# Turning the stationary and moving operands of the value product round in the later batches of a banded attention + MLP kernel

## The chip, the cores and the metric

One core of a Trainium2 chip runs the whole program. The metric is the device time of one execution in microseconds (us). The core's engines work side by side, each through its own instruction list in order: TensorE (PE; its weight loads are shown apart, as PEld), VectorE (DVE), ScalarE (ACT), GpSimd (POOL) and SyncE (SP), which issues the DMAs. Matmul results land in PSUM, eight banks of 512 fp32 columns.

## The reference

Attention over 8 batches, 8 heads, 576 positions and 64 head dimensions: each query sees 32 keys, the last 32 in heads 0 to 3 ("plain"), every fourth of the last 128 in heads 4 to 7 ("dilated"). Then a two-layer perceptron over the 4608 rows of 512.

```python
scores = scale * np.matmul(q, k.transpose(0, 1, 3, 2))
mask_plain = (rel >= 0) & (rel < window)
mask_dil = (rel >= 0) & (rel < window * dilation) & (rel % dilation == 0)
...
attn = np.exp(scores - max)
attn = attn / (np.sum(attn, axis=-1, keepdims=True) + 1e-09)
x = np.matmul(attn, v)          # heads side by side: 4608 x 512
...
h = x @ w_in                    # 512 -> 2048
g = np.maximum(0.01 * h, h)
return g @ w_out                # 2048 -> 512
```

## The kernel before

**A list written by a planner.** Every piece of work is a task with an engine, an estimated duration, dependencies and a priority (a due time). `_Plan.run` plays these tasks through and fixes the order in which each engine gets its instructions; the chip then runs each engine's list in order. Batches 0 and 1 are "early" and go another way than batches 2 to 7 ("late", `b >= EARLY`), which the change is about.

**Attention of a late batch.** Heads go in pairs, four pairs (`hp`) to a batch: 2 and 3 dilated, 0 and 1 plain. `load_group` loads q, k and v and casts them to fp16 (POOL); `turn` transposes q and k with DVE (L562, L573) and spreads q with POOL (L567) into `slots`. Then `unit` handles a third of a pair, 384 score columns, three units to a pair:

- scores, keys on partitions and queries in columns: 2 matmuls of 192 columns (L742), or in the small dilated unit 4 of 96 (L726), into the one bank `sps`;
- the exponential on ACT, PSUM to `ee` (L748), and the 0/1 mask on DVE (L762);
- the values: v with 64 columns of ones beside it (128 columns) is the **stationary** operand, the exponentials are **moving**, 4 matmuls of 96 columns (L806) or 8 of 48 (L796). Partitions 0 to 63 of `ops` then hold the unnormalised x with its dimensions on partitions, and partitions 64 to 127 hold the sum of each column, 64 times over;
- the reciprocal of the sums as two ACT instructions over 64 x 384, Ln (L818) and Exp of the negative (L820);
- DVE multiplies and writes into `xt` (L824): two instructions of 64x192 in a plain unit, one of 64x384 in a dilated one.

**The perceptron** works on `chunks` of 384 columns of `xt`, three to a pair of batches. `up` (L851): 16 results per chunk, each 4 matmuls of 384 columns into one of two `hps` banks, each taken away by ACT with the leaky ReLU (L862). The second layer takes 128-row tiles: the first four as plain products (L903), the other 32 in eight groups of four by a scheme of seven products instead of eight (`group`, L993), with sums of the inputs by DVE (L979), evictions by ACT (L1022) and result sums by DVE (L1030). A group uses three cells X, Y and Z, each one bank, out of `fps0`, `fps1` and the `tp` bank; `roles` exchanges the two `fps` banks from group to group. The last group (`split`) has six banks.

**PSUM**: `tp`, two `ops`, two `hps`, `sps`, two `fps`.

Of the kernel before, what the change touches and what calls it, by code (L numbers as in the profile page):

```python
# [23 lines left out]
def _constants():  # L24

    ident = np.eye(128, dtype=np.float16)
    p = np.arange(128)[:, None]
    key = p - 32
    c = np.arange(96)[None, :]
    qry = 4 * (c % 24) + c // 24  # L30
    rel = qry - key
    band = (rel >= 0) & (rel < WIN)
    first = band & (key >= 0)
    rel0 = c - p
    d0 = (rel0 >= 0) & (rel0 < WIN)
    c1 = np.arange(48)[None, :]
    rel1 = 96 + c1 - (16 + p)
    d1 = (rel1 >= 0) & (rel1 < WIN)
    rel2 = 96 + c1 - np.where((p < 64) & (p % 4 == 0), 128 + p // 4, p)
    d2 = (rel2 >= 0) & (rel2 < WIN)  # L40
    masks = np.concatenate([first, band, band, d0, d1, d2], axis=1)
    parts = [ident, np.where(masks, 0.0, -60000.0), masks]
    return np.concatenate([x.astype(np.float16) for x in parts], axis=1)
# [17 lines left out]
class _Plan:  # L61
# [22 lines left out]
    def run(self):  # L84
        free, waiting = {}, {}
# [13 lines left out]
        while len(order) < len(self.tasks):  # L99
# [19 lines left out]
            t.eng, t.start, t.dur = eng, at, dict(t.choices)[eng]  # L119
            free[eng] = at + t.dur  # L120
# [17 lines left out]
def kernel(  # L138
# [10 lines left out]
    nc = tc.nc  # L149
# [39 lines left out]
    NMASK = 288 + 96 + 48 + 48  # L189
    NCON = 128 + 2 * NMASK  # L190
    con = sbuf("con", [128, NCON])
    ident = con[:, 0:128]
    M_PL, M_D0, M_D1, M_D2 = 128, 128 + 288, 128 + 288 + 96, 128 + 288 + 96 + 48
    w_in = sbuf("w_in", [128, NI * DFF])
    w_out = sbuf("w_out", [128, NJ * DM])
    NST, NNAT, NVS, NV, NT, NE, NR, NO, NG = 5, 3, 2, 3, 6, 4, 3, 3, 3
# [3 lines left out]
    vst = [sbuf(f"vst{i}", [128, 2048], FP32) for i in range(NVS)]  # L200
# [6 lines left out]
    ee = [sbuf(f"ee{i}", [128, 384]) for i in range(NE)]  # L207
    rc = [sbuf(f"rc{i}", [128, 384], FP32) for i in range(NR)]
# [8 lines left out]
    t4 = sbuf("t4", [128, 2048])  # L217
# [6 lines left out]
    tpb = bank("tp", FP16)  # L224
    ops = [bank(f"ops{i}") for i in range(2)]
    hps = [bank(f"hps{i}") for i in range(2)]
    banks = {"S": [bank("sps0")], "O": ops}
# [50 lines left out]
    t_bias = load("ACT", con[:, 128:128 + NMASK], const_d[:, 128:128 + NMASK], 128, 2 * NMASK, [],  # L278
                  -1498.5)
    t_con = load("SP", con[:, 128 + NMASK:NCON], const_d[:, 128 + NMASK:NCON], 128, 2 * NMASK, [],  # L280
# [45 lines left out]
    def load_group(b, g, prio, prio_v):  # L326
# [26 lines left out]
        vn, v_old = ring("VST", NVS, v_users := [])  # L353
        vs = vst[vn]
        if dil and early:
            lv = [load("SP", at(vs, 0, 128, 0, [256, 4], [1, 256]),
                       dram(v, base, [4 * D, 128], [HS, 4], [1, 256]), 512, 1024, v_old, prio_v)]
            v_late[b] = vs, v_old, v_users
        elif dil:
            lv = [load("SP", at(vs, 0, 128, i * 256, [512, 4], [1, 256]),  # L360
                       dram(v, base + i * 64 * D, [4 * D, 128], [HS, 4], [1, 256]),
                       512, 1024, v_old, prio_v) for i in range(2)]
        elif early:
            lv = []
            for j in range(2):
# [7 lines left out]
                lv.append(lj)  # L373
        else:
            lv = [load("SP", at(vs, 0, 128, 0, [D, 24], [1, D]),
                       dram(v, base - 32 * D, [D, 128], [96 * D, 24], [1, D]),
                       3072, 256, v_old, prio_v)]

        for j in range(2):
            nn, n_old = ring("NAT", NNAT, n_users := [])  # L380
            na, c_qk = nat[nn], []
            for o in range(2):
# [5 lines left out]
                else:  # L388
# [8 lines left out]
            h_a, h_s = (2 * j * n_v, n_v) if early else (j * n_v, 2 * n_v)  # L397
            n, w = n_v // D, 128 * (8 if dil else 6)
            c_v = [cast(at(vt, 0, 128, 0, [w, 2], [128, n], [1, D]),
                        at(vs, 0, 128, h_a, [h_s, 2], [D, n], [1, D]), 2 * n_v,  # L400
                        (lv[j] if early and not dil else lv) + d_old, prio_v)]
            v_users += c_v
# [70 lines left out]
    segs = {b: [(0, 96, 384 * (b % 2)), (96, 48, 768 + 192 * (b % 2))] for b in range(B)}  # L473
    chunks = [(m, 384 * i, 384) for m in range(B // 2) for i in ((0, 1, 2) if m < 3 else (0, 2, 1))]
# [8 lines left out]
    def chunk_at(m, x):  # L483
        return next(c for c, (mc, xc, n) in enumerate(chunks) if mc == m and xc <= x < xc + n)

    def pieces(b, hp, u, tiled):
# [7 lines left out]
        for u0, nu, base in segs[b]:  # L494
# [14 lines left out]
            if dil and b >= EARLY:  # L509
                p0 = h0 % 2 * 64  # L510
                res.append((key, 0, 64,
                            at(xm, p0, p0 + 64, h0 // 2 * 1152 + x, xs[0], [1152, 2], xs[1]), 0,
                            [cs[0], [step // 2, 2], cs[1]]))
                continue
# [22 lines left out]
    held = {t.name: [] for t in banks["S0"] + banks["O0"]}  # L537
# [8 lines left out]
    def turn(b, hp, part, prio):  # L546
# [11 lines left out]
        if b >= EARLY:  # L558
# [5 lines left out]
            for hh in range(2):  # L564
                p0 = 64 * hh
                t = add("POOL", 0.72, 0.2, [tq] + old + zq,
                        lambda e, p0=p0, hh=hh: nc.gpsimd.tensor_copy(  # L567
                            out=at(qb, p0, p0 + 64, hh * S + o, *od),
                            in_=at(xb, p0, p0 + 64, i, *id_)), prio)
                x_users.append(t)  # L570
                ev.append(t)
# [123 lines left out]
    def unit(b, hp, part, u, turned, prio):  # L695
# [11 lines left out]
        if sk == "S0":  # L707
            held[st.name].append(s_users)
            held[ot.name].append(o_users)
# [4 lines left out]
        def scores(e):  # L714
            if by_pe:
                if small:
                    bias = at(con, 0, 128, M_D2, [0, 8], [1, 48])
                elif dil:
                    bias = at(con, 0, 128, M_D0, [0, 4], [1, 96])
                else:  # L720
                    bias = at(con, 0, 128, M_PL + (0 if u == 0 else 96),
                              [96, 2], [0, 2], [1, 96])
                nc.tensor.matmul(st[:, 0:384], ident, bias, start=True, stop=False)
            if small:
                for s in range(4):
                    nc.tensor.matmul(  # L726
                        st[:, 96 * s:96 * s + 96],
                        (at(kb, 0, 128, s * 144, [1, 128]) if b < EARLY
                         else at(kb, 0, 128, PAD + s + 4 * 16, [4, 128])),
# [3 lines left out]
            for i in range(2):  # L733
                t = 2 * u + i
                if dil:
                    ka = (at(kb, 0, 128, t * 144, [1, 128]) if b < EARLY
                          else at(kb, 0, 128, PAD + t, [4, 128]))
# [14 lines left out]
        def mask(e):  # L752
            if small:
                mk = at(con, 0, 128, NMASK + (M_D2 if b < EARLY else M_D1), [0, 8], [1, 48])
                io = at(et, 0, 128, 0, [48, 8], [1, 48])
            elif dil:
                mk = at(con, 0, 128, NMASK + M_D0, [0, 4], [1, 96])
                io = at(et, 0, 128, 0, [96, 4], [1, 96])
            else:
                mk = at(con, 0, 128, NMASK + M_PL + (0 if u == 0 else 96), [96, 2], [0, 2], [1, 96])  # L760
# [7 lines left out]
        def values(e):  # L768
# [23 lines left out]
            if small:  # L792
                for s in range(4):
                    for hh in range(2):
# [3 lines left out]
                            at(vt, 0, 128, (hh * 8 + 4 * (b >= EARLY) + s) * 128, [1, 128]),  # L798
# [23 lines left out]
        for key, p0, p1, dst, c, i_ in pieces(b, hp, u, tiled):  # L822
# [3 lines left out]
            t_n = add("DVE", 0.61 if dil and b >= EARLY else 0.38, 0.2,  # L826
# [5 lines left out]

    gt_free = {1 - NG: sum(w_used[11:14], []), 2 - NG: w_used[0] + w_used[1]}

    def up(c, j, x, n, done, acc):

        m, x0, n_c = chunks[c]
        if c == 0 and j in WIDE:
            h_users = []
            ht, name, x_r = {2: (fps[1], "F", -1), 3: (banks["S"][0], "S", -1), 4: (ops[0], "O", 0),  # L840
                             5: (ops[1], "O", 1), 6: (tpb.bitcast(FP32), "TP", -1)}[j]
# [6 lines left out]
        def pe(i0, i1):  # L848
            def fn(e):
                for i in range(i0, i1):  # L850
                    nc.tensor.matmul(ht[:, 0:n],  # L851
                                     at(w_in, 0, 128, i * DFF + j // 2 * 256 + j % 2, [2, 128]),
                                     at(xt[m % 2], 0, 128, i * 1152 + x0 + x, [1, n]),
# [16 lines left out]
    def rows(c, tt):  # L870

        m, x0, n = chunks[c]
        res = []
        for p in range(128):
            x = x0 + tt * 128 + p
# [52 lines left out]
    def weight_sums():  # L928
# [7 lines left out]
        minus(4, flat(sums[4]), w_block(1, 0), flat(sums[2]), [t_sum[2]])  # L936
        minus(3, w_block(0, 1), w_block(1, 1), w_block(0, 1), [t_sum[1]] + plain_parts)

    roles = [0, 1]
# [3 lines left out]
    def group(four, acts, at_time, split):  # L943
# [15 lines left out]
        if split:  # L959
            cells = [[(b, 0) for b in pair] for pair in (fps, [trio[2], banks["S"][0]], ops)]  # L960
            pairs = ((0,), (1,))
            room = {fps[0].name: last_of[fps[0].name], fps[1].name: last_of[fps[1].name],
                    trio[2].name: last_of[trio[2].name], banks["S"][0].name: rings["S"][-1],
                    ops[0].name: rings["O"][-2], ops[1].name: rings["O"][-1]}
        else:
            three = [trio[i] for i in roles] + [trio[2]]
            roles.reverse()
            cells = [[(b, HN * i) for i in range(2)] for b in three]
            pairs = ((0, 1),)
            room = {b.name: last_of.get(b.name, first_banks.get(b.name, [])) for b in trio}  # L970
# [6 lines left out]
        def add_up(dst, a, b, op, deps, who, t_late=0.0):  # L977
            t = add((("DVE", 0.66), ("POOL", 2.3)), None, 0.2, deps,
                    lambda e: ENG[e].tensor_tensor(out=dst, in0=a, in1=b, op=op),  # L979
# [5 lines left out]
        def product(src, rhs, cell, first, deps, when, who=None):  # L985
            ts = []
            for i in range(2):
# [9 lines left out]
                old = room.get(bk.name, []) if first else []  # L997
# [35 lines left out]
        def result(make, deps, pair, row, col):  # L1033
            if split:
                r = (row + col) * 2 + pair[0]
                ob, o_old, o_users = vst[0][:, r * HN:r * HN + HN], rings["VST"][-2], []
# [12 lines left out]
        def flat8(i):  # L1049
# [12 lines left out]
        p7 = product(raw(2, 0), lambda j: w_out[:, j * DM + HN:j * DM + DM], Z, True,  # L1062
                     lambda i: [s3[i], t_sum[3]], 2, 2)

# [7 lines left out]
        p6 = product(raw(0, 0), w_sum(2), X, False, lambda i: [s2[i], t_1[i], t_sum[2]], 3, 0)  # L1072
# [24 lines left out]
        if not split:  # L1097
            for b, t in zip(three, (c12, c11, c21)):
                last_of[b.name] = [t[0]]
# [3 lines left out]
    trio = [fps[0], fps[1], tpb.bitcast(FP32)]  # L1103
# [25 lines left out]
    def release():  # L1129

        def users(t):
            return sum(held[t.name], [])
# [4 lines left out]
    def attend(b, part, first, step):  # L1137
        units = {None: (0, 1, 2), 0: (0, 1), 1: (2,)}[part]
        if part == 1:
            load_rest(b, ranks[b])  # L1140
        for n, hp in enumerate((2, 3, 0, 1)):
# [3 lines left out]
            got = turn(b, hp, part or 0, first + step * n)  # L1145
            for u in units:
                unit(b, hp, part or 0, u, got, first + step * n)
# [3 lines left out]
    for m in range(B // 2):  # L1151
# [14 lines left out]
        while n_c < len(chunks) and chunks[n_c][0] == m:  # L1166
# [11 lines left out]
            if n_c == 2:  # L1178
# [5 lines left out]
                for i in range(2):  # L1184
                    first_banks[fps[i].name] = rings["F"][i - 2]
                first_banks[trio[2].name] = rings["TP"][-1]
# [60 lines left out]
```

## Time and profile before

| what | value |
|---|---|
| time, median of 3 runs (lowest, highest) | 315.37 us (313.8, 317.77) |
| the profiled execution: its own time, its span | 316.78 us, 315.0 us |
| mean granted TensorE clock in it | 0.994 |
| DMA | 51.2 MB in 163,395 packets, 140,448 of them under 512 bytes |
| q, k and v of the late batches | 96 loads of 144 KB, 12 of 512 KB, 6 of 768 KB |

The profile is one execution. Busy time of PE is modelled: a matmul's record runs from its start to the arrival of its last result, so records overlap and a busy PE is not yet a PE at its full rate. The full rate shows in the distance between the starts of neighbouring matmuls. In the chain of waits each row has a start, a length and what ran.

### The profile page before, as it was taken

Reading aid. Unit: us, or ns where it says so; the run is one execution under the profiler, and the core shown is the slowest. Engines: PE = TensorE matmul, PEld = TensorE weight load, DVE = VectorE, ACT = ScalarE, POOL = GpSimd, SP = SyncE. Lnnn points to the kernel's source line nnn. Section 1 sums busy time; section 2 is a strip of 40 time slices with the busy share of each in tenths; the row PEclk is TensorE's granted clock in tenths of the full one; section 3 lists DMA queues with packets and bytes.
Section 4 is the critical chain, followed back from the end, with each engine's and each line's share of the span. In section 5 each row is a group of like instructions: output and inputs, shape, how many; then the busy total and the mean of one; then the engine's idle time right before and its main releaser. Section 6 shows DMA issues by size and latency. Waiting matters only on the chain.

```text
span 315.0 us, 7276 instructions
## 1 busy us (share of the span) xinstructions
PE 297.0 (94%) x2622; PEld 216.2 (69%) x2622; DVE 222.7 (71%) x453; ACT 231.9 (74%) x534; POOL 133.9 (43%) x175
## 2 busy tenths in 40 slices
PE   7996999799889998899999999999899999999995
PEld 3644554467778786688777777787687777767784
DVE  5844899755988999987979878779956442151172
ACT  3934864589998899789899998699697885454421
POOL 3558655563564767455655747957200000000000
PEclk9999999799999999999999999999999999999999
DMA  7999999999599932899599978796203010130223
GB/s 252 343 332 397 403 295 197 246 174 205 180 173 200 233 60 73 163 188 245 114 220 184 195 184 140 187 182 168 58 10 92 4 34 2 45 91 0 57 79 100
DMA packets 163395, 51.20 MB, mean 163 GB/s; under 512 B 140448, under 2 KB 160800, under 8 KB 163360
## 3 DMA queue, kind: packets, MB, share of 16 engines
q1 hardware_dynamic: 162336, 50.01, 66.6%
q10 hardware_dynamic: 1024, 0.75, 0.8%
q8 instruction: 20, 0.33, 0.4%
q14 instruction: 15, 0.12, 0.1%
HBM read 41.30 MB, written 9.44 MB: 161 GB/s over the span
## 4 chain that ended last, share of the span: by engine, by line
PE 61%; DVE 14%; DMA 7%; SPq 6%; ACT 6%; issue 4%; DVEq 0%; ACTq 0%
PE hps L851 29%; PE fps L993 18%; SPq L248 6%; PE tp L993 6%; DMA wst<-in_moe_w_in_dram 3%; DVE xt L824 3%; ACT gt L862 3%; DMA stg<-in_q_dram 3%; PE ops L806 2%; PE sps L742 2%; DMA stg<-in_k_dram 2%; DVE slots L532 2%; DVE gt L979 2%; DVE ee L762 2%; DVE rest L979 1%
## 5 line engine op out<-in xcount | busy, mean ns | idle before, releaser
L851 PE MATMUL hps<-xt,w_in 128*128 128x384 f16 (+1 forms) x812 | 149.2, 316 | 5.7 <-ACT gt L862 1.9
L862 ACT ACTIVATE gt<-hps 128x384 f16<-128x384 f32 (+1 forms) x203 | 92.3, 461 | 35.9 <-PE hps L851 33.6
L851 PEld LDWEIGHTS <-w_in 128*128 128x128 f16 x832 | 77.0, 98 | 42.6 <-issue 7.7
L993 PEld LDWEIGHTS <-gt 128*128 128x128 f16 x768 | 73.5, 98 | 12.2 <-DVE gt L979 0.7
L824 DVE TENSOR_TENSOR xt<-ops,rc 64x192 f16<-64x192 f32 (+2 forms) x138 | 52.1, 397 | 24.0 <-ACT rc L820 19.3
L567 POOL COPY slots<-turned 64x576 f16<-64x576 f16 x48 | 36.0, 749 | 52.0 <-DVE turned L562 50.4
L818 ACT ACTIVATE rc<-ops 64x384 f32<-64x384 f32 (+1 forms) x94 | 43.5, 464 | 12.9 <-PE ops L806 4.0
L748 ACT ACTIVATE ee<-sps 128x384 f16<-128x384 f32 x92 | 44.7, 485 | 8.6 <-PE sps L742 4.4
L258 POOL CAST nat<-stg 128x576 f16<-128x576 f32 (+1 forms) x53 | 42.0, 816 | 13.0 <-DMA stg<-in_k_dram 6.5
L993 PE MATMUL fps<-w_out,gt 128*128 128x256 f16 x368 | 47.5, 273 | 0.0
L820 ACT ACTIVATE rc<-rc 64x384 f32<-64x384 f32 (+1 forms) x96 | 46.5, 491 | 1.1
L762 DVE TENSOR_TENSOR ee<-ee,con 128x384 f16<-128x384 f16 x79 | 38.4, 492 | 12.5 <-ACT ee L748 12.0
L1030 DVE TENSOR_TENSOR osb<-tp,stg 128x512 f32<-128x512 f32 x14 | 9.6, 686 | 25.0 <-ACT stg L1022 16.8
L742 PE MATMUL sps<-slots 128*128 128x192 f16 x152 | 25.0, 246 | 0.9 <-DVE slots L532 0.8
L258 POOL CAST vd<-vst 128x1024 f16<-128x1024 f32 (+2 forms) x20 | 19.2, 983 | 6.6 <-DMA vst<-in_v_dram 6.4
L742 PEld LDWEIGHTS <-slots 128*128 128x128 f16 x160 | 15.4, 102 | 8.1 <-DVE slots L532 1.4
L1022 ACT COPY stg<-fps 128x512 f32<-128x512 f32 (+1 forms) x26 | 13.9, 534 | 9.4 <-PE fps L993 9.3
L532 DVE COPY slots<-tp 64x128 f16<-64x128 f16 (+7 forms) x43 | 13.6, 333 | 7.2 <-PE tp L580 6.7
L573 DVE STREAM_TRANSPOSE slots<-nat 128x576 f16<-128x576 f16 x24 | 18.0, 762 | 0.7 <-POOL nat L258 0.6
L562 DVE STREAM_TRANSPOSE turned<-nat 128x576 f16<-128x576 f16 x24 | 18.1, 762 | 0.1
L979 DVE TENSOR_TENSOR gt<-gt 128x1024 f16<-128x1024 f16 x21 | 17.2, 838 | 0.8 <-PE fps L993 0.7
L993 PE MATMUL fps<-wst,gt 128*128 128x256 f16 x128 | 16.4, 273 | 0.0
(102 smaller groups left out, 317.6 us busy)
## 6 DMA issues: line engine op xcount, KB each, us to landing
vst<-in_v_dram SPq DMA_DIRECT2D x14, 512.0 KB, 4.8
stg<-in_q_dram SPq DMA_DIRECT2D x48, 144.0 KB, 3.3
stg<-in_k_dram SPq DMA_DIRECT2D x48, 144.0 KB, 2.9
vst<-in_v_dram SPq DMA_DIRECT2D x6, 768.0 KB, 5.6
gt<-in_moe_w_in_dram SPq DMA_DIRECT2D x5, 512.0 KB, 8.3
out_dram<-osb SPq DMA_DIRECT2D x22, 96.0 KB, 2.0
out_dram<-osb SPq DMA_DIRECT2D x44, 48.0 KB, 1.7
out_dram<-osb SPq DMA_DIRECT2D x27, 64.0 KB, 2.6
```

The lines of the kernel that those rows point to most:

```text
L258: ENG[e].tensor_copy(out=dst, in_=src)
L567: lambda e, p0=p0, hh=hh: nc.gpsimd.tensor_copy(out=at(qb, p0, p0 + 64, hh * S + o, *od), in_=at(xb, p0, p0 + 64, i, *id_)), prio)
L742: nc.tensor.matmul(st[:, 192 * i:192 * i + 192], ka, qa, start=not by_pe, stop=i == 1 or not by_pe)
L748: lambda e: nc.scalar.activation(out=et, in_=st[:, 0:384], func=AF.Exp, scale=SCALE), prio + 0.1)
L762: ENG[e].tensor_tensor(out=io, in0=io, in1=mk, op=ALU.mult)
L818: lambda e: nc.scalar.activation(out=r_out, in_=r_in, func=AF.Ln), prio + 0.2)
L820: lambda e: nc.scalar.activation(out=r_out, in_=r_out, func=AF.Exp, scale=-1.0),
L824: nc.vector.tensor_tensor(out=dst, in0=at(ot, p0, p1, c, *i_), in1=at(rt, p0, p1, c, *i_), op=ALU.mult)
L851: nc.tensor.matmul(ht[:, 0:n], at(w_in, 0, 128, i * DFF + j // 2 * 256 + j % 2, [2, 128]), at(xt[m % 2], 0, 128, i * 1152 + x0 + x, [1, n] ...
L862: lambda e: nc.scalar.activation(out=gt[c % NG][:, j * n_c + x:j * n_c + x + n], in_=ht[:, 0:n], func=AF.Prelu, alpha=0.01),
L979: lambda e: ENG[e].tensor_tensor(out=dst, in0=a, in1=b, op=op),
L993: nc.tensor.matmul(bk[:, x:x + HN], tl[:, off + j * step:off + j * step + 128], rhs(j), start=first and x == 0 and j == 0, stop=j == HJ - ...
```

## The change

For late batches `unit` gives way to `late_unit`, two units of 576 columns to a head pair instead of three of 384, and to `across`, once per group of two pairs. `unit`, with its old operand order, stays for batches 0 and 1.

- The scores of a unit go into two banks (`s_two`, the old `sps` and `tp`), in 6 matmuls of 96 columns (plain) or 2 of 192 and 2 of 96 (dilated). One exponential and one mask cover 576 columns.
- In the value product the **exponentials are stationary** (96 columns: 96 queries) and **v with one column of ones moves** (65 columns). Queries are now on partitions, and the sum is the 65th column. A plain unit has 6 such matmuls, a dilated one 8.
- DVE takes the reciprocal of 96 x 6 sums and multiplies 96 x 384 results with it into `xnat`.
- When a group of four heads is done, `across` turns `xnat` with 12 TensorE transposes (128 stationary columns, 96 moving) into the `ops` banks, and four moves a batch (ACT or DVE, as the planner finds) of 128 x 576 take them to `xt`.
- Without the `tp` bank, a group of the second layer has X on `fps0` and both Y and Z on `fps1`; p7 comes after p6 and waits for the result sum c11 that empties Y.
- v is loaded by head pair in half-size staging slots (8 loads a batch instead of 3, the same bytes), three slots of 1024 columns instead of two of 2048; one of the weight sums moves into that memory.
- `xt` holds a batch's 576 columns together, so a chunk of the third kind reads two runs of 192. Sums of the second layer are planned on DVE alone; the planner lets DVE and POOL work delay one another.

```diff
-    tpb = bank("tp", FP16)
-    ops = [bank(f"ops{i}") for i in range(2)]
+    s_two, o_two = (ps.tile([128, 1024], FP32, name=n) for n in ("sps", "ops"))
+    sps0, tpf = s_two[:, 0:512], s_two[:, 512:1024]
...
+        def values(e):
+            def one(t, hh, c, k, first, last):
+                r = 65 * (2 * t + hh)
+                nc.tensor.matmul(ot[0:96, r:r + 65], et[:, c:c + 96],
+                                 at(vt, 0, 128, (hh * (8 if dil else 6) + k) * 128, [1, 65]),
+                                 start=first, stop=last)
+            for t in range(3):
+                for hh in range(2):
+                    if not dil:
+                        one(t, hh, 288 * hh + 96 * t, 3 * n + t, True, True)
+                    elif t < 2:
+                        one(t, hh, 336 * hh + 240 * t, 2 * n + t, True, True)
+                    else:
+                        one(t, hh, 336 * hh + 96, 4 + 2 * n, True, False)
+                        one(t, hh, 336 * hh + 144, 5 + 2 * n, False, True)
...
+        t_r = add("DVE", 0.13, 0.15, [t_v] + c_old,
+                  lambda e: nc.vector.reciprocal(out=rt[0:96, :], in_=at(ot, 0, 96, 64, [65, 6])),
+                  prio + 0.2)
+        def norm(e):
+            nc.vector.tensor_tensor(
+                out=at(xb, 0, 96, 768 * n + 64 * i, [256, 3], [128, 2], [1, D]),
+                in0=at(ot, 0, 96, 0, [130, 3], [65, 2], [1, D]),
+                in1=at(rt, 0, 96, 0, [2, 3], [1, 2], [0, D]), op=ALU.mult)
...
+    def across(b, g, prio):
+        for i in range(2):
+            def pe(e, i=i, tb=tb):
+                for t in range(6):
...
+                    nc.tensor.transpose(to, xb[0:96, 256 * t + 128 * i:256 * t + 128 * i + 128],
+                                        ident[0:96, 0:96])
+            t_x = move(dst, tb[:, 0:S], S, [t_t] + x_free.get(m, []), prio + 0.2, ("ACT", "DVE"))
...
-            three = [trio[i] for i in roles] + [trio[2]]
-            roles.reverse()
-            cells = [[(b, HN * i) for i in range(2)] for b in three]
+            cells = [[(b, HN * i) for i in range(2)] for b in (*fps, fps[1])]
...
-        p6 = product(raw(0, 0), w_sum(2), X, False, lambda i: [s2[i], t_1[i], t_sum[2]], 3, 0)
+        p6 = product(raw(0, 0), w_sum(2), X, False, lambda i: [s2[i], t_1[i], t_sum[2]], 2, 0)
+        p7 = product(raw(2, 0), lambda j: w_out[:, j * DM + HN:j * DM + DM], Z, True,
+                     lambda i: [s3[i], t_sum[3]], 3, 2,
+                     after=None if split else [c11[0]])
```

## The prediction

> **What bounds the kernel now.** I read the page first. By the shares of busy time PE leads, with ACT and DVE near each other behind it:
>
> ```profile
> PE 297.0 (94%) x2622; PEld 216.2 (69%) x2622; DVE 222.7 (71%) x453; ACT 231.9 (74%) x534; POOL 133.9 (43%) x175
> ...
> PE   7996999799889998899999999999899999999995
> ...
> PEclk9999999799999999999999999999999999999999
> ```
>
> A modelled 94% does not say at what rate PE works, and the stages differ, so I cut the span into windows of 25 us. The columns are the window, its length, busy us (instructions) of PE, PEld, DVE, ACT and POOL, the granted clock, the DMA share and GB/s:
>
> ```profile
> 75.00:100.00 25.00, 22.69 (x253) 19.56 (x250) 21.85 (x42) 23.51 (x68) 14.40 (x19) 1.00 0.89 182
> 100.00:125.00 25.00, 24.84 (x235) 19.04 (x233) 24.03 (x41) 23.05 (x53) 17.07 (x21) 1.00 0.62 131
> 125.00:150.00 25.00, 23.32 (x219) 17.89 (x217) 21.98 (x42) 21.11 (x47) 12.97 (x18) 1.00 0.94 193
> 150.00:175.00 25.00, 24.96 (x227) 18.39 (x225) 22.44 (x39) 23.22 (x53) 13.32 (x16) 1.00 0.91 184
> 175.00:200.00 25.00, 25.00 (x230) 19.48 (x228) 21.01 (x44) 21.64 (x49) 17.95 (x19) 1.00 0.83 156
> ```
>
> From 75 to 225 us late attention and perceptron share the engines, with ACT at 84 to 94% and DVE at 82 to 96%. Third came the chain of waits in order of time, which shows both the rates and the one stretch where PE really stops:
>
> ```profile
> 81.66 0.66 PE hps L851 x8
> 82.32 0.17 PE sps L742 x2
> 82.49 0.87 PE fps L993 x8
> 83.36 0.21 PE ops L796 x8
> ...
> 86.20 0.32 ACT gt L862
> 86.52 0.04 issue
> 86.56 0.49 PE hps L851 x4
> 87.05 0.22 PE sps L742 x2
> 87.27 0.17 PE ops L806 x4
> ```
>
> Eight matmuls of 256 columns take 0.87 us, two of 192 columns 0.17, four of 96 columns 0.17, eight of 48 columns 0.21: PE starts a matmul every 109, 83, 42 and 26 ns, about 0.43 ns a column, and the narrowest not under 25 ns. At 86.2 PE waits for ACT to empty an `hps` bank. Taking each matmul's columns at that rate away from the distance to the next start leaves PE's true gaps (those over 0.1 us): 4.3 us in 50 to 75, 4.3 in 75 to 100, 3.0 in 100 to 150, 0.2 in 150 to 225, 1.7 in 225 to 250, 0.4 later; 13.9 us after 50 us. From 150 us on, apart from one gap, PE runs at its full column rate: **there only PE's own work counts, and an ACT instruction saved is worth nothing.** The change is worth what it takes out of the 13.9 us, less what it adds to PE.
>
> Last, the rows by form, for prices (busy us, mean ns of one, then idle before):
>
> ```profile
> L748 ACT ACTIVATE ee<-sps 128x384 f16<-128x384 f32 x92 | 44.7, 485 | 8.6 <-PE sps L742 4.4 <-PE sps L726 3.6
> L820 ACT ACTIVATE rc<-rc 64x384 f32<-64x384 f32 x80 | 41.2, 516 | 0.9
> L818 ACT ACTIVATE rc<-ops 64x384 f32<-64x384 f32 x80 | 38.9, 487 | 8.7 <-PE ops L806 4.0 <-PE ops L796 2.8
> L762 DVE TENSOR_TENSOR ee<-ee,con 128x384 f16<-128x384 f16 x79 | 38.4, 492 | 12.5 <-ACT ee L748 12.0
> L824 DVE TENSOR_TENSOR xt<-ops,rc 64x192 f16<-64x192 f32 x88 | 27.8, 344 | 13.3 <-ACT rc L820 12.7
> L824 DVE TENSOR_TENSOR xt<-ops,rc 64x384 f16<-64x384 f32 x36 | 19.7, 547 | 9.5 <-ACT rc L820 5.6 <-PE ops L796 1.8 <-PE hps L851 1.5
> L806 PEld LDWEIGHTS <-vp 128*128 128x128 f16 x160 | 11.0, 98 | 4.2 <-issue 2.2
> L786 PEld LDWEIGHTS <-vp 128*64 128x64 f16 x32 | 1.4, 108 | 2.2 <-issue 1.2 <-DVE slots L532 0.4 <-POOL vp L258 0.4
> ```
>
> **The change part by part**, for one late batch (four pairs), times 6.
>
> *ACT.* Removed: 12 units x (485 + 487 + 516 ns) = 17.9 us. Added: 8 exponentials of 576 columns; 192 columns of an ACT pass cost about 0.33 us and 384 about 0.49, so 0.65 each, 5.2 us; and up to 4 moves of 576 at about 0.65 (the ACT copy of 128x512 fp16 took 0.59), 2.6. Net 10.1 to 12.7 less a batch, 61 to 76 us in all, off the path from 150 us on.
>
> *DVE.* Removed: 12 masks x 0.492 + 12 x 0.344 + 6 x 0.547 = 13.3 us. Added: 8 masks of 576 (between 0.54, from the 0.36 that an undisturbed mask takes, and 0.74; I take 0.65) 5.2; 8 reciprocals of 6 columns (between the 0.07 of a small memset and the 0.17 of a 64x32 copy out of PSUM; 0.17) 1.4; 8 products of 96x384 at the 0.55 of the same shape on 64 partitions 4.4. Net 2.3 less, or nothing if all four moves fall to DVE at 0.6.
>
> *PE, the term that decides.* Scores: before 20 x 83 + 8 x 42 ns = 2.0 us; after 24 x 42 + 8 x 83 + 8 x 42 = 2.0. Nothing.
> Values: before, plain 6 x 0.17, dilated 4 x 0.17 + 2 x 0.21: 2.12 us. After, 56 matmuls of 65 columns. By columns they take 27 ns each, 1.51 us: over 6 batches a gain of 3.7. But each needs a fresh stationary of 96 columns, and no row has that. The nearest: 128-column loads keep up with a matmul every 26 ns; the 64-column loads of batch 0 show a *longer* record (108 ns against 98), and where one could not hide (a load issued at 8.721, its matmul started at 8.761) it took 40 ns. So a narrow load is not a cheaper one; for 96 columns the bounds are 27 (hidden) and 60 (40 scaled by columns), and I take 50, nearer to the row with a narrow load. The first load of a unit hides under the matmul before: 4 x (5 x 50 + 27) + 4 x (7 x 50 + 27) = 2.62 us; +3.0 us over 6 batches (bounds -3.7 and +5.9).
> [...] No run here shows a 96-column load yet.
> Transposes: 24 a batch with 96 moving columns; the transposes of 128 columns start every 56 ns, so 42 by columns: 1.0 us a batch, **+6.1 us** (bounds 6.1 and, at 56 ns, 8.1). Their stationary is 128 columns wide.
> PE sum: 0 + 3.0 + 6.1 = **+9.1 us**, bounds +2.4 and +14.0. None of it has cover: PE is full.
>
> *The gaps.* 75 to 100: the stalls are for `hps` banks behind Ln and Exp on a full ACT; a batch's 17.9 us of ACT become 7.8, so I take back 4.0 of 4.3. 50 to 75: 1.9 at 57.5 us is a mask of batch 1, untouched, and much of the rest is the wait for q and k (DMA share 1.07 there); 1.0 of 4.3. 100 to 150: DVE is late (1.6 us at 126.9, behind a 2.65 us sum slowed beside POOL work); 2.0 of 3.0. 225: 1.0 of 1.7. Sum **-8.0 us** (bounds 0 and -13.9); what is late next is DVE.
>
> *Bank for the second layer.* p7 now waits for c11, the next group's p1 for c12 and p2 for c21. The waiting instruction holds everything behind it on PE. Cover: c11 is ready 0.16 us (a 384-column record lasts 0.33, its successor starts after 0.16) + 0.69 (the L1030 sum) after p2 if DVE is free, and p6 runs 1.74 us meanwhile; the others have the same 1.74 from a product between. Cost 0 while DVE is less than 0.9 us behind; beyond that each wait is PE time.
>
> *Rest.* POOL, q and k: the same count. v: 8 loads instead of 3, some 0.6 us of issue each on SP, 3 us more a batch on a queue that is ahead of need except in 50 to 75 us; 0, and up to 1 us of that stage's recovery if not. Memsets, constants, the new column order of `xt`: the same matmuls and stores, 0.
>
> **Sum.** +9.1 - 8.0 = +1.1 us on the profiled execution (span 315.0, own time 316.78, 0.4% above the median). On the median: 315.4 + 1.1 = **316.5 us**.
>
> **Rivals.**
> - *The narrow load hides after all* (27 ns, as the 128-column ones do), and a lighter ACT and DVE close most gaps: +2.4 - 10.5, **307.3 us**. For it: the load of the next stationary starts with the matmul before it all over the trace. Against: the 40 ns.
> - *Slower: the two-bank groups.* DVE at 96% in 100 to 125 us runs sums of up to 2.65 us ahead of an L1030; with a backlog over 0.9 us c11, c12 and c21 stop PE. At 1.2 us a group over the 7 groups, +8.4: **325 us**. Against it: uprojections stand between the products and give more cover.
> - *ACT is relieved for nothing*: the planner puts the moves on DVE, DVE stays at 19.4 us a batch, and the gaps from 100 on stay: +9.1 - 5.0, **319.5 us**.
>
> **How the numbers follow.** Forecast 0.40 (own range 312 to 321.5), narrow load hidden 0.27, two-bank groups 0.22, DVE as before 0.11. A change of under 2%, 6.3 us, is about what a measurement of this kernel can't tell from none: faster means under 309.1, slower over 321.7. Faster: 0.24 of the first rival and 0.02 of the forecast, 0.26. Slower: 0.19 + 0.08 + 0.04 = 0.31. Within: 0.43. The range runs from 306, just under the first rival, to 326, just over the second.
>
> **What would show it.** [...] Wrong would be the whole account if PE shows true gaps after 150 us, where I take it as full.

## The result, and the profile after

| | median us (lowest, highest) | profiled execution: own time, span | clock |
|---|---|---|---|
| before, run beside it | 315.53 (313.8, 317.77) | 316.78, 315.0 | 0.994 |
| changed | 337.43 (334.72, 339.84) | 336.5, 334.7 | 0.994 |

The ratio is 1.066, 95% interval 1.055 to 1.077: slower by 21 us, against a forecast of +1.1 us and a range that ended at 326. Times and ratios from here on are of fast runs alone, since one run of the changed kernel (339.84 us) and one of experiment 2 (319.8 us) were slow ones; the changed kernel's median is 336.5 us by them. The page of the changed kernel (busy us, share of the span, instructions; then busy tenths in 40 slices):

```profile
PE 307.3 (92%) x2839; PEld 225.1 (67%) x2839; DVE 206.5 (62%) x428; ACT 178.1 (53%) x380; POOL 129.7 (39%) x176
...
PE   7887878999999999999999898968999999999974
...
PEclk9999979999999999999999999999999999999999
```

ACT went from 74% to 53% of the span, DVE from 71% to 62%, and still the time rose. The digits of PE show where to look: before, they stood at 8 or 9 from a quarter of the span to its last slice; now one, at 220 us, is 6. The windows of 25 us place it:

```profile
75.00:100.00 25.00, 23.78 (x276) 19.70 (x275) 19.71 (x41) 16.93 (x44) 14.77 (x19) 1.00 1.18 176
100.00:125.00 25.00, 24.95 (x271) 20.52 (x271) 21.05 (x38) 16.39 (x35) 16.48 (x21) 1.00 1.07 164
125.00:150.00 25.00, 24.90 (x253) 19.60 (x252) 17.96 (x39) 14.06 (x28) 12.78 (x17) 1.00 0.91 141
150.00:175.00 25.00, 24.81 (x243) 18.20 (x241) 16.04 (x32) 16.21 (x33) 12.40 (x16) 1.00 0.90 163
175.00:200.00 25.00, 23.83 (x236) 18.54 (x235) 16.78 (x34) 13.25 (x26) 13.46 (x18) 1.00 1.18 165
200.00:225.00 25.00, 20.65 (x204) 16.23 (x202) 18.39 (x31) 10.81 (x21) 12.07 (x15) 1.00 0.93 159
```

From 75 to 150 us the change did what it was to do: PE is busier than before at 75 to 100 and 125 to 150, on a much lighter ACT. From 175 to 225 us PE idles, and no compute engine is near full: DVE has 16.8 and 18.4 of 25 us, ACT 13.3 and 10.8. What is high is the share of the DMA engines (the last but one column): 1.18 at 175 to 200 us for 165 GB/s, where the kernel before had 0.83 for 156. The chain of waits there, in order of time (start, length, what ran):

```profile
194.09 5.38 DMA stg<-in_k_dram
199.47 0.02 issue
199.49 0.04 POOLq L271
199.53 0.08 issue
199.62 0.67 POOL nat L271
200.29 0.02 issue
200.31 0.78 DVE slots L601
201.09 0.77 DVE el L919
201.86 0.04 issue
201.90 0.55 PE ops L926 x8
```

A load of k takes 5.38 us to land. The cast on POOL, DVE's transpose, the mask behind it in DVE's list and the value matmuls on PE then follow one another with nothing between: PE waits for a transfer. The page's parts on the DMA queue and its issues (packets, MB, share of 16 engines; KB each, median us to landing) say the same of the whole run. Before:

```profile
q1 hardware_dynamic: 162336, 50.01, 66.6%
...
stg<-in_q_dram SPq DMA_DIRECT2D x48, 144.0 KB, 3.3
stg<-in_k_dram SPq DMA_DIRECT2D x48, 144.0 KB, 2.9
```

and after:

```profile
q1 hardware_dynamic: 162816, 50.05, 76.8%
...
stg<-in_q_dram SPq DMA_DIRECT2D x48, 144.0 KB, 4.5
stg<-in_k_dram SPq DMA_DIRECT2D x48, 144.0 KB, 4.6
```

The same bytes in nearly the same number of packets, the same loads of q and k, and yet 22% more DMA time (76.8% of 334.7 us against 66.6% of 315.0) and landings 1.2 to 1.7 us later. By packet size the mean went from 12.9 to 17.7 ns (128 bytes) and from 18.0 to 23.7 ns (256 bytes); the median of the 128-byte packets stayed at 13 ns, but 30% of them now took over one and a half times that. Something makes a part of the packets slow.

PE's time can be split as in the prediction, into its work (each matmul at the distance to the next start that its kind shows) and its true gaps over 0.1 us:

| us | before | changed | change |
|---|---|---|---|
| PE's work | 282.5 | 290.6 | +8.1 |
| gaps, 0 to 50 us | 10.6 | 15.8 | +5.2 |
| gaps, 50 to 150 us | 11.5 | 7.7 | -3.8 |
| gaps, 150 us to the end | 2.3 | 11.1 | +8.8 |

So the question is not PE's work, which is near the +9.1 foretold, but 14 us of new gaps, at the start and after 150 us.

### The profile page after: what moved, and what is told of

It is laid out like the page before. It is cut to its first block, busy times and chain, and to the rows that moved or that the text cites. A ratio compares the mean times of both kernels' runs of the same rounds, so it can differ in the third digit from the quotient of the medians.

```text
span 334.7 us, 7436 instructions
## 1 busy us (share of the span) xinstructions
PE 307.3 (92%) x2839; PEld 225.1 (67%) x2839; DVE 206.5 (62%) x428; ACT 178.1 (53%) x380; POOL 129.7 (39%) x176
## 3 DMA queue, kind: packets, MB, share of 16 engines
q1 hardware_dynamic: 162816, 50.05, 76.8%
q10 hardware_dynamic: 1024, 0.73, 0.8%
## 4 chain that ended last, share of the span: by engine, by line
PE 55%; DMA 12%; SPq 12%; DVE 8%; ACT 5%; issue 4%; POOL 2%; DVEq 0%; POOLq 0%; ACTq 0%
PE hps L1007 24%; PE fps L1146 20%; SPq L261 12%; DMA stg<-in_k_dram 7%; DMA stg<-in_q_dram 5%; PE ops L926 3%; DVE slots L560 2%; POOL nat L271 2%; DVE xt L850 1%; PE ops L974 1%; ACT gt L1018 1%; ACT ee L774 1%; PE sps L897 1%; PE ops L1146 1%; PE fps L1059 1%
## 5 line engine op out<-in xcount | busy, mean ns | idle before, releaser
L1146 PEld LDWEIGHTS <-gt 128*128 128x128 f16 x768 | 74.1, 98 | 16.2 <-DVE gt L1132 2.1
L1146 PE MATMUL fps<-w_out,gt 128*128 128x256 f16 x480 | 61.9, 273 | 0.0
L1183 DVE TENSOR_TENSOR osb<-fps,stg 128x512 f32<-128x512 f32 x21 | 14.3, 682 | 27.2 <-ACT stg L1175 15.4
L948 DVE TENSOR_TENSOR rc<-ops,rec 96x384 f16<-96x384 f32 x48 | 25.9, 543 | 2.3 <-PE ops L926 1.6
L601 DVE STREAM_TRANSPOSE slots<-nat 128x576 f16<-128x576 f16 x24 | 17.9, 755 | 9.6 <-POOL nat L271 9.6
L271 POOL CAST vd<-v_all 128x1024 f16<-128x1024 f32 (+2 forms) x20 | 18.5, 940 | 7.6 <-DMA v_all<-in_v_dram 6.8
L560 DVE COPY slots<-sps 64x128 f16<-64x128 f16 (+7 forms) x43 | 13.6, 334 | 12.4 <-PE sps L608 6.5
L271 POOL CAST vp<-v_all 128x768 f16<-128x768 f32 x16 | 15.2, 951 | 15.1 <-DMA v_all<-in_v_dram 13.1
L905 ACT ACTIVATE el<-sps 128x576 f16<-128x576 f32 x24 | 15.6, 652 | 4.5 <-PE sps L890 4.4
L905 ACT ACTIVATE ee<-sps 128x576 f16<-128x576 f32 x24 | 15.6, 649 | 4.3 <-PE sps L897 4.1
L774 ACT ACTIVATE ee<-sps 128x384 f16<-128x384 f32 x20 | 9.8, 489 | 14.3 <-DVE slots L560 6.0
L1132 DVE TENSOR_TENSOR gt<-gt 128x1024 f16<-128x1024 f16 x21 | 15.8, 770 | 1.6 <-PE fps L1146 1.6
L1059 PE MATMUL fps<-w_out,gt 128*128 128x512 f16 x64 | 16.4, 384 | 0.2 <-DVE osb L1067 0.2
```

The source lines that it names most:

```text
L271: ENG[e].tensor_copy(out=dst, in_=src)
L560: nc.vector.tensor_copy(out=dst, in_=src)
L601: lambda e: nc.vector.transpose(kb[:, PAD:PAD + S], na[:, S:2 * S]), prio)
L905: lambda e: nc.scalar.activation(out=at(et, 0, 128, 0, *dims), in_=at(s_two, 0, 128, 0, *s_dims), func=AF.Exp, scale=SCALE), prio + 0.1)
L948: nc.vector.tensor_tensor(out=at(xb, 0, 96, 768 * n + 64 * i, [256, 3], [128, 2], [1, D]), in0=at(ot, 0, 96, 0, [130, 3], [65, 2], [1, D]) ...
L1059: nc.tensor.matmul(ft, g[:, j * n_c + tt * 128:j * n_c + tt * 128 + 128], w_out[:, j * DM:j * DM + DM], start=(j == 0), stop=(j == NJ - 1))
```

## Two causes, and their rivals

**The addresses.** The tile `con` of constants is the first of the program's tiles in on-chip memory. In the changed kernel it has 96 more columns (it holds other masks), so it is 2368 bytes a partition long instead of 2176, and every tile behind it is shifted by 192 bytes. The staging tiles in which q, k and v land began at a multiple of 256 bytes before and begin 192 bytes behind one now. Then every packet of 256 bytes lies across a multiple of 256, and every second one of 128 bytes. The rival: the new pattern of the v loads (eight instead of three a batch), or a planner's order that sends transfers into one another.

**The tiles.** Before, `sps`, `tp` and the two `ops` banks were four tiles. The changed kernel makes two of them: `s_two` holds the old `sps` and `tp`, `o_two` both `ops` banks. The waits that the program carries are set per tile, so an instruction on one bank may have to wait for a user of the other. This stretch of the changed kernel's timeline (start, length, engine, line, what it writes and reads, idle time before and its releaser) shows it:

```profile
13.57 0.36 DVE L560 COPY slots<-sps 64x384 f16<-64x384 f16 x1
...
13.99 0.32 PE L751 MATMUL sps<-con 128*128 128x384 f16 x1 [0.55 <-DVE slots L560]
```

The copy reads the half of the tile that was `tp` (before, its row says `slots<-tp`), the matmul writes the other half, and PE stands still for 0.55 us until the copy has ended. In the program's instruction list the matmul of L751 carries a wait for DVE; with separate tiles (the experiment of four tiles, below) the same matmul carries none for DVE. The rival is that these waits lie where PE would have waited anyway.

## The experiments

All medians are of runs on the chip that also ran the kernel before (314.6 to 316.0 us). Experiments ran on several chips, so a difference of 1 us between two of them says little unless the ratios to before say the same.

**1. The addresses alone, in both directions.** `con` is moved behind the tiles that DMAs fill, with the 128-byte tile `ones` at its old place, so that the staging tiles of q, k and v start at multiples of 256 again. Every engine's instruction list is the same as in the changed kernel.

```diff
-    con = sbuf("con", [128, NCON])
-    ident = con[:, 0:128]
+    ones = sbuf("ones", [128, D])
...
+    con = sbuf("con", [128, NCON])
+    ident = con[:, 0:128]
```

> The constants tile (8 bytes x 24 larger in the change, 192 bytes a partition) is moved behind the other tiles, so that the staging tiles lie at multiples of 256 bytes again, as before the change; nothing else. Theory A (the 192-byte shift of every DMA destination slows the packets): 128-byte packets back from a mean of 17.7 to 13 ns, PE's gaps before 50 us back from 15.8 to about 10.6 us and those in 175 to 250 us from 8.5 to about 1; time 322 to 327, that is the 315.5 of before plus the 8.5 us of PE work less some gaps. Theory B (the new pattern of the v loads, or another load on the chip, slows them): packets stay at 17 to 18 ns, time 334 to 339.

Measured: 329.1 us, ratio to before 1.043 (1.037 to 1.049), 7.4 us less than the changed kernel and above the 322 to 327 expected. Packets are back at 12.9 and 17.9 ns, queue q1 at 64.3%, gaps after 150 us at 4.7 us instead of 11.1. The gaps before 50 us did not move (15.3 us); that part of the expectation was a miss, and it is not the addresses'.

The other direction is the kernel before with 192 bytes of padding in `con`, nothing else; again every instruction list is unchanged but for the longer row of `con`:

```diff
-    con = sbuf("con", [128, NCON])
+    con = sbuf("con", [128, NCON + 96])
```

> The kernel before, its constants tile lengthened by 192 bytes, so that all later tiles move as far as the change moved them; no instruction differs. Theory A: 128-byte packets 17 to 18 ns instead of 12.9, time 322 to 332, the loss standing before 50 us and in the late attention. Theory B: 12.9 ns, 315 to 316 us.

Measured: 329.65 us, ratio 1.045 (1.039 to 1.051), **13.7 us for 192 unused bytes**. Packets took 16.9 and 23.6 ns, and PE has gaps of 3.8 us at 200 to 225 us and 3.0 at 225 to 250, where the kernel before has 0 and 1.7. This kernel has the old loads and the old order, so neither is needed for the loss. The shift moves the operands of the compute engines too, but their work takes as long as before: the median cast of 128x576 on POOL took 0.67 us in both, and ACT's instructions add up to 255.8 and 255.9 us.

Two sizes of the shift were compared later, 128 bytes against 192:

```diff
-    con = sbuf("con", [128, NCON])
+    con = sbuf("con", [128, NCON + 64])
```

> The kernel before, its constants tile lengthened by 128 bytes: the q, k and v staging tiles begin 128 bytes after a multiple of 256 instead of on it (e2: 192 after). A 128-byte packet then never lies across a multiple of 256, a 256-byte one always does. If crossing a multiple of 256 is what costs: 128-byte packets 13 ns, 256-byte packets 23 or more, time 316 to 320. If any start off a multiple of 256 costs: 128-byte packets 17 ns, time 325 to 330. If only starts off a multiple of 128 cost: nothing changes, 315 to 316.

Measured: 317.82 us, ratio 1.006 (1.004 to 1.008). At 128 bytes past the multiple a 128-byte packet doesn't cross it, and took 13.3 ns; a 256-byte packet does, and took 20.5. This lies between the two plain answers. Packets that don't cross a multiple of 256 are seldom slow here: 6% of the 128-byte ones took over 13 ns, against 36% at 192 bytes, where every second one crosses, and 1% before. But crossing alone isn't the rule. All 256-byte packets cross at 128 and at 192, and 34% of them took over 18 ns at the one, 64% at the other. A start off a multiple of 128 may count as well; no run parts the two. Only the destinations of the transfers moved in these runs; how that makes packets longer was not shown.

**2. Do the stores gain by the same rule?** `xt`, `gt` and the output staging `osb` start 128 bytes behind a multiple of 256 in the kernel before. One tile was moved to bring them to a multiple.

```diff
+    ones = sbuf("ones", [128, D])
     ee = [sbuf(f"ee{i}"
```

> The kernel before, with a 128-byte tile moved so that the weight landing places (gt, xt) and the output tiles (osb) begin at multiples of 256 instead of 128 after one. If long packets pay for crossing too: 4096-byte packets from a mean of 173 to 160 ns, 1 to 2 us off the first 50 us, about 314 us. If not: 315 to 316.

Measured: 315.67 us, ratio 0.998 (0.995 to 1.000). No gain that matters. The same on the best version of the changed kernel (number 5 below):

> As e7, with gt, xt, osb and wst at multiples of 256 too. By the same question: 312.5 to 313.5, or the 314 of e7.

Measured: 315.4 us, ratio 0.999 (0.997 to 1.002), no better than without. Nor were the stores from `osb` slower to land in the changed kernel: medians of 1.8 to 2.1 us for the four commonest sizes, against 1.7 to 2.6 before.

**3. PE's terms by themselves.** Both go on top of the aligned kernel of number 1 (329.1 us). First the stationary operand is widened to 128 columns wherever the tile has them (all but one matmul of each dilated unit); the extra rows of the result are not used.

```diff
+                w = 128 if c + 128 <= (672 if dil else 768) else 96
-                nc.tensor.matmul(ot[0:96, r:r + 65], et[:, c:c + 96],
+                nc.tensor.matmul(ot[0:w, r:r + 65], et[:, c:c + w],
```

> As e1, with 128 stationary columns loaded instead of 96 in all value matmuls but one of a dilated unit; the 32 more rows of the result are not read. If a 96-column load is what sets the 45 ns between these matmuls, they go to 27 ns: 300 of them x 18 ns = 5.4 us of PE, time 5 us under e1. If the distance comes from the 65 moving columns or the PSUM writes, 45 ns and the time of e1.

Measured: 326.52 us, ratio 1.034 (1.029 to 1.039), 2.6 us less. The distance between starts fell from 45 to 29 ns, and PE's work from 290.5 to 286.3 us; the gaps took part of the 4.2 us back (27.2 to 29.2 us), but 2.4 us of them stand in 6.8 us at half clock, which the aligned kernel's trace doesn't have. So loading **more** columns is faster: the record of a 96-column load is 122 ns long in this run, that of a 128-column load 97 to 100.

Then each transpose of `across` is done twice:

```diff
-                for t in range(6):
+                for t in [*range(6), *range(6)]:
```

> As e1, with each of the 144 TensorE transposes done twice into the same place. If PE's own work sets the time of the late attention, +144 x 42 ns = +6 us over e1. If the loads or DVE still set it, +0 to +3.

Measured: 335.66 us, ratio 1.064 (1.059 to 1.069), +6.6 us for 144 more transposes, 46 ns each where the trace has 42 between starts. The transposes lie on the path in full.

**4. The tiles.** On the aligned kernel, the two `ops` banks become two tiles again. Each engine's instruction list has the same operations in the same order; only waits differ.

```diff
-    s_two, o_two = (ps.tile([128, 1024], FP32, name=n) for n in ("sps", "ops"))
+    s_two = ps.tile([128, 1024], FP32, name="sps")
...
-    ops = [o_two[:, 512 * i:512 * i + 512] for i in range(2)]
+    ops = [bank(f"ops{i}") for i in range(2)]
```

> As e1, with the two ops banks as two tiles again instead of two halves of one; no instruction differs, only which instructions wait for which. Theory C (waits are set per tile, so that two banks in one tile wait for each other's users): PE's gaps before 50 us from 15.3 to 12 or 13 us, the gap of 1.9 us at 213 us shorter, time 2 to 4 us under e1. Rival D (the early loss of 4.7 us comes from the planner's new order and the longer constants load): the time of e1.

Measured: 322.05 us, ratio 1.023 (1.016 to 1.029), 7.0 us less by waits alone, where 2 to 4 were expected. From 100 us to the last group only 0.76 us of gaps are left. Then `sps` and `tp` are parted as well. A 576-column exponential can't cover two tiles, so it becomes two of 288, and the planner's order changes a little with it:

```diff
-    sps0, tpf = s_two[:, 0:512], s_two[:, 512:1024]
+    sps0, tpf = bank("sps0"), bank("tp")
+    s_two = [sps0, tpf]
...
+            for y in range(2):
+                nc.scalar.activation(
...
+                    in_=s_two[y][:, 0:288] if not dil else at(s_two[y], 0, 128, 0, [144, 2], [1, 144]),
```

> As e5, with the two score banks as two tiles again too; the one late exponential of 576 columns becomes two of 288 (about 0.4 us each instead of 0.65, 48 units, +7 us of ACT, which is 54% busy). Theory C: gaps before 50 us at 10 to 11 us as in the kernel before, first uprojection at 17 us instead of 19.8, time 4 to 7 us under e1 in all. Rival D: the time of e1.

Measured: 318.61 us, ratio 1.010 (1.007 to 1.013), another 3.4 us less, although ACT has 50 instructions more than in the changed kernel. Gaps before 50 us are back at 10.55 us (before: 10.6), all gaps at 16.7 (before: 24.4). The windows of this kernel, to be held against those of the changed one:

```profile
150.00:175.00 25.00, 25.00 (x255) 19.23 (x253) 19.10 (x38) 17.15 (x41) 14.80 (x18) 1.00 0.94 188
175.00:200.00 25.00, 25.00 (x244) 19.82 (x243) 17.72 (x36) 14.13 (x32) 11.28 (x16) 1.00 0.84 177
200.00:225.00 25.00, 25.00 (x240) 19.75 (x239) 17.42 (x31) 14.21 (x33) 11.40 (x15) 1.00 0.59 126
```

PE is full, on the same transfers. The reverse was run too: the kernel before with its four banks put into two tiles, each list again with the same operations in the same order.

```diff
-    tpb = bank("tp", FP16)
-    ops = [bank(f"ops{i}") for i in range(2)]
+    s_two, o_two = (ps.tile([128, 1024], FP32, name=n) for n in ("sps", "ops"))
+    sps0, tpf = s_two[:, 0:512], s_two[:, 512:1024]
+    tpb = tpf.bitcast(FP16)
+    ops = [o_two[:, 512 * i:512 * i + 512] for i in range(2)]
...
-    banks = {"S": [bank("sps0")], "O": ops}
+    banks = {"S": [sps0], "O": ops}
```

> The kernel before, with sps and tp as two halves of one tile and the two ops banks as two halves of another, and nothing else. Theory C: slower by 4 to 8 us, gaps before 50 us at about 15 us and more PE waits in the late attention. Rival D: 315 to 316 us.

Measured: 341.78 us, ratio 1.081 (1.075 to 1.088): **+26 us for two names**, where 4 to 8 were expected. The table of waits (who waits for whom: us in total, times, longest) of the kernel before has

```profile
PE ops L806 <- DVE xt L824: 1.2, 1, 1.2
```

and that of the merged one, where the lines stand two lower,

```profile
PE ops L808 <- DVE xt L826: 10.1, 17, 1.4
...
PE sps L725 <- DVE slots L534: 3.3, 5, 1.5
```

The value matmuls wait for DVE's reading of the `ops` tile 17 times instead of once: double buffering is gone.

**5. Together.** Four tiles, aligned, and the wide stationary:

> As e6, with the 128-column stationary loads of e3. If the two add up: 2.5 to 4 us under e6, about 319 us; 315.5 is not reached, since the transposes stay.

Measured: 314.11 us over ten runs, ratio 0.996 (0.9924 to 0.9995), the best of the versions tried. The expectation that 315.5 would not be reached was wrong, but this is level with the kernel before rather than faster: the near copy of experiment 2, with the same instruction lists, came to 0.999. Its page and two rows of its chain of waits:

```profile
PE 297.7 (95%) x2839; PEld 219.4 (70%) x2839; DVE 205.0 (66%) x426; ACT 181.5 (58%) x430; POOL 129.5 (41%) x176
```

```profile
105.89 0.26 PE ops L931 x8
...
112.88 0.18 PE ops L931 x6
```

Eight value matmuls took 0.34 us in the changed kernel and take 0.26 here.

**6. Do the two causes add?** The last run is the changed kernel at its own addresses, with the four tiles alone. Its instruction lists are those of the aligned kernel with four tiles (318.61 us).

> The changed kernel with its address layout as it is (staging tiles 192 bytes behind a multiple of 256), and only the four banks (sps, tp and the two ops banks) given a tile each. If the two causes add, the 10.5 us that the split took from e1 (329.1 to 318.6) come off 337.4: 326 to 329 us. If they overlap (the packets that land late also hold up what the shared tiles hold up), less comes off: 331 to 335. If the shared tiles were most of the loss and the addresses only matter through them, under 325. In each case the true gaps of TensorE after 150 us (9.8 us in the changed kernel) show it: near 5 if the packets alone still make them, under 2 if the tiles made them.

Measured: 336.26 us, ratio 1.068 (1.065 to 1.071), where the changed kernel has 1.066. Nothing clear of the noise came off, less than any of the three cases allowed; gaps after 150 us are 12.3 us (11.1 in the changed kernel, by the same count). They don't add:

| median us | staging 192 bytes off | staging aligned | difference |
|---|---|---|---|
| two shared tiles (the change) | 336.5 | 329.1 | 7.4 |
| four tiles | 336.3 | 318.6 | 17.7 |
| difference | 0.2 | 10.5 | |

While the packets are slow, taking waits away upstream makes PE arrive earlier at the next late load: against the changed kernel, gaps before 75 us fell from 20.1 to 13.1 us, and those from 100 to 175 us rose from 1.0 to 9.8. The slow packets reach PE by a second way too. In the trace of this run (the timeline):

```profile
123.29 4.12 SPq L261 DMA_DIRECT2D out_dram<-osb  x8
...
126.44 0.69 DVE L1187 TENSOR_TENSOR osb<-fps,stg 128x512 f32<-128x512 f32 x1 [4.04 <-DMA out_dram<-osb]
...
127.48 0.55 DVE L952 TENSOR_TENSOR rc<-ops,rec 96x384 f16<-96x384 f32 x1
...
128.09 0.90 PE L978 MATMUL ops<-con,rc 96*128 96x96 f16 x9 [4.37 <-DVE rc L952]
```

SP issues loads and stores from one list. Its issues of the 144 loads of q, k and v for the late batches took 127.2 us in all here, 109.5 in the aligned kernel with the same list. The stores behind them came late (that the longer issues alone made them so is a reading of this one place), DVE's sum L1187 waited 4.04 us for its output buffer, the product L952 stood behind that sum in DVE's list, and PE waited 4.37 us for it.

PE's clock has a part in this run as well. Its page shows slices below 9:

```profile
PEclk9999989999999995999999999989999999999999
```

The granted clock was half for 13.7 us of this trace in three stretches, for 3.4 us in the changed kernel's, and nowhere inside that of the aligned kernel with four tiles. The second stretch begins at 127.0 us, within the 4.37 us wait above, and lasts 6.8 us; the third begins at 222.6 us, 1.2 us behind a wait of 3.0 us for a load of k that took 6.07 us. In all three, matmuls start 5.9 us later than at their usual distances, against 1.7 us in the changed kernel. So some 4 us of this run's time is the slower clock (an estimate from these two figures); at an equal clock the four tiles would have taken about that much off, still less than 10.5. All four runs have a mean clock of 0.980 to 0.983, while the kernel before had 0.998 to 1.000 on the same chip. Whether the waits bring the lower clock on was not tested; in this trace two of the three stretches come after or within one. The shifted kernel before of experiment 1 shows the same order once: a wait of 2.3 us until 211.4 us, then half clock from 212.1 to 215.5.

## Why the prediction failed, step by step

**PE's work: right, with the parts a little off.** The 65-column matmuls start every 45 ns; the prediction took 50, with bounds of 27 and 60. (The 40 ns that it scaled from were not the load alone: the 96-column matmul ahead had started only 63 ns before, and such a matmul takes 42.) The chain of waits of the changed kernel shows both new kinds:

```profile
106.72 0.34 PE ops L926 x8
...
116.65 0.51 PE ops L974 x12
...
119.85 0.26 PE ops L926 x6
```

Six in 0.26 us, eight in 0.34, twelve transposes in 0.51 (42 ns each, as foretold). At 45 ns the values cost +1.5 us instead of +3.0, and the transposes +6.1; the measured total is +8.1 for +9.1. The prediction's argument, that a narrow load is not a cheap one, held: the record of a 96-column load is 124 ns long here, that of a 128-column load 98, and in experiment 3 the distance between starts is 45 ns with 96 columns and 29 with 128. The rival in which the narrow load hides fell; it needed 27.

**ACT and DVE: right.** The rows by form, for the prices that were taken (busy us, mean ns of one, idle before):

```profile
L948 DVE TENSOR_TENSOR rc<-ops,rec 96x384 f16<-96x384 f32 x48 | 25.9, 543 | 2.3 <-PE ops L926 1.6
L905 ACT ACTIVATE ee<-sps 128x576 f16<-128x576 f32 x24 | 15.6, 649 | 4.3 <-PE sps L897 4.1
L919 DVE TENSOR_TENSOR ee<-ee,con 128x576 f16<-128x576 f16 x24 | 13.5, 565 | 5.1 <-ACT ee L905 5.0
L926 PEld LDWEIGHTS <-el 128*96 128x96 f16 x192 | 11.4, 124 | 4.3 <-DVE el L919 1.9 <-issue 0.7 <-DVE xt L560 0.4
L558 ACT COPY xt<-ops 128x576 f16<-128x576 f16 x14 | 8.9, 641 | 6.0 <-PE ops L974 4.2 <-DVE xt L560 1.8
L944 DVE RECIPROCAL rec<-ops 96x6 f32<-96x6 f32 x48 | 8.4, 182 | 16.4 <-PE ops L926 14.8 <-ACT stg L1175 1.3
```

0.55 was taken for the product and 0.543 came, 0.65 for exponential and move (0.649 and 0.641), 0.65 for the mask (0.565), 0.17 for the reciprocal (0.182). DVE's busy time fell by 16.2 us, 2.7 a batch for the 2.3 foretold. ACT's fell by 53.8; the 61 to 76 of the forecast were summed durations, which fell by 65.7 (ACT's records overlap). From 150 us on ACT's relief had nothing to buy, as the prediction said: the gaps there were 2.3 us before.

**The bank for the second layer: right.** Cost 0. With four tiles no gap after 125 us is left but the one before the last group (1.9 us, where the first product waits for DVE's input sums; 0.4 before). The rival of two-bank groups, 325 us, fell, though the changed kernel came out on its side; so did the one in which ACT is relieved for nothing, since the gaps from 100 to 150 us fell from 3.0 to 0.5 in the changed kernel itself.

**The gaps, -8.0: missed in the changed kernel, near in another, in part by luck.** In the changed kernel all gaps together rose by 10.1. With aligned staging and four tiles they fell from 24.4 to 16.7, by 7.7:

| us | forecast | changed | aligned, four tiles |
|---|---|---|---|
| PE's work | +9.1 | +8.1 | +7.9 |
| gaps | -8.0 | +10.1 | -7.7 |
| span, profiled execution | +1.1 | +19.7 | +0.7 |
| median | 316.5 | 336.5 | 318.6 |

The last column flatters the forecast. The traced execution of the kernel before spent 58.8 to 62.2 us at half clock (the 7 in its PEclk row); the count of gaps has 1.5 us of that, and the prediction took it for waiting. The traced execution with four tiles has no such stretch. The medians on one chip differ by 2.9 us (318.6 and 315.7), not by 0.7. The split by stage was less good than the sum: 50 to 75 us gave 3.4 (1.0 foretold), 75 to 100 gave 2.5 (4.0), 100 to 150 gave 1.5 (2.0), 225 gave 1.7 (1.0), and the last group lost 1.5 that was not foretold.

**The step that failed** is the paragraph "Rest": "Memsets, constants, the new column order of `xt`: the same matmuls and stores, 0." The constants' tile is 192 bytes longer, and its length sets the address of every DMA destination behind it. That costs 13.7 us in the kernel before and 7.4 to 17.7 us here. The trace of before couldn't have priced it, since all its staging of q, k and v is aligned, but the address could have been worked out from the changed code.

The second omission stands in the same place: the merging of four banks into two tiles is in the diff, and the prediction gave it no line. It counted banks and what fills and empties each, as if waits were set by bank. The waits are set by tile, and the price is 10.5 us with aligned addresses (7.0 of it by the `ops` tile with no other difference), 26 us in the kernel before, and nothing that could be measured while the packets were slow. The prediction's own test, true gaps of PE after 150 us, showed at once that the account was wrong.

What stays open: how the packets' lateness is made inside the DMA engines, why only a part of the crossing packets is slow, what part the clock has in the losses, and how much of the 3.4 us between three tiles and four is the planner's new order, since the two can't be parted there.

## What to carry to other kernels

When a change alters the size of any tile, work out where the tiles behind it begin: start the tiles in which small DMA packets land at a multiple of 256 bytes (192 bytes behind one cost 13.7 us here, 128 bytes 1.9), and try moving a tile first, since it changes no instruction. Before two buffers are merged into one tile for the sake of one wide instruction, ask what each half waits for: where waits are kept by tile, the merged pair is no longer a double buffer (26 us in the kernel before, 10.5 us in the aligned one). Try widening a stationary operand of 96 columns to 128 when there is memory behind it to read, even if the extra results are thrown away: it took off 2.6 and 4.5 us here.

## What the runs showed of the hardware that was not expected

- DMA destinations 192 bytes behind a multiple of 256 made 128-byte packets 12.9 to 16.9 ns and 256-byte packets 18.0 to 23.6 ns long (means) with the same program, +13.7 us on 316; 128 bytes behind made them 13.3 and 20.5 ns, +1.9 us on 315.9. The median 128-byte packet stayed at 13 ns.
- With 65 moving columns, matmuls with a 96-column stationary start every 45 ns, those with 128 columns every 29 ns.
- With four tiles at the changed addresses, PE's granted clock fell to half for 6.8 us from within a wait of 4.37 us on, and for 3.4 us from 1.2 us behind one of 3.0 us.
